# Loading weight tiles, and the queries and keys of attention units, in halves

## The chip, the cores and the metric

The kernel runs on one core of one Trainium2 chip. The metric is the device time of one execution in microseconds (us). It was run three times: 1044.6 us median, 1043.4 to 1045.1. A separate profiled execution gives the trace. Its engines are TensorE (PE in the rows, PEld for its weight loads), VectorE (DVE), ScalarE (ACT), GpSimd (POOL) and SyncE (SP), which here issues the DMA transfers.

## The reference

Attention in chunks over 4 batches, 8 heads, 768 positions and 64 channels a head; its output goes through two feed-forward layers of 3072 tokens, 512 model channels and 2048 hidden ones. All in float32:

```python
for c in range(nc):                      # chunks of 32 queries
    k_full = concat([mem_k, k[l_start:r_end]])   # 8 memory keys, 16 left, 32, 8 right
    scores = scale * q_c @ k_full.T
    a = exp(scores - max(scores)); a = a / (sum(a) + 1e-09)
    out[c] = a @ v_full
x = out as [3072, 512]
h = x @ w_in;  x = (h * clip(h + 3, 0, 6) / 6) @ w_out        # first layer
h = x @ w_in2; out = maximum(0.01 * h, h) @ w_out2            # second layer
```

## The kernel before

Every float32 product of the layers is made of three passes on TensorE: an operand is cut into a high and a low part, and high by high, high by low and low by high are summed. The weights arrive as 64-bit patterns of 128 x 512 numbers (512 KB a tile); "decode" reads one into a "w" buffer in a single transfer (line 393) and rebuilds the float on ACT (line 396) and DVE (lines 400, 404, 408). There are 64 such tiles, 16 for each of the four weight matrices. For much of the work, blocks of 512 tokens are taken in pairs and multiplied in seven products instead of eight, with sums of weights and of tokens that are formed on the way and kept in DRAM ("kept1i", "kept2i", "kept1o", "kept2o").

Attention is done in units: a unit is half a batch of one group of four heads. Its queries and keys come in two transfers of 448 KB (function "load_qk" in "unit", line 491), each with two groups of 96 queries: 128 rows, two runs of 448 numbers in each. The first units of the second half batch are cut into half units (function "half_unit", line 769). The keys are copied into windows (line 341), then follow the scores on TensorE (line 544), the greatest (561), the exponent on ACT (580), the sum (593, 594), the norm on DVE or POOL (598), the transposes on TensorE (602) and the product with the values (622, 634). The first units run before there is anything for the layers; the later ones are placed between matmuls of the first layer.

The order of all this is not written by hand. Each step is a task with a cost per engine, a key, the buffers that it takes and the tasks that it follows. The function "schedule" runs through a model of the engines in time and hands out the tasks; each engine then executes its instructions in the order so found. For a DMA the model books 500 ns of SP for each transfer that the task says it issues ("issues"), at most eight transfers on their way (LANES), and the bytes on one wire. In the built program, too, SP uses eight semaphores in turn (DMAHW0 to DMAHW7): a transfer that takes a semaphore waits for the one eight before it. Buffers are few: "st" has two, "ys" four, "wm" two.

Of the kernel before, what the change touches and what calls it, by code (L numbers as in the profile page):

```python
# [9 lines left out]
F32 = mybir.dt.float32  # L10
F32R = mybir.dt.float32r
U32 = mybir.dt.uint32
# [5 lines left out]
B, H, S, D, NMEM = 4, 8, 768, 64, 8  # L18
# [5 lines left out]
QK = 2 * G + 2 * KW  # L24
# [32 lines left out]
RATE_QK, RATE, RATE_V, COLD = 380.0, 220.0, 300.0, 1.1  # L57
# [198 lines left out]
def tile_attn_moe_moe2(ctx: ExitStack, tc: tile.TileContext, raw, w1i, w1o, w2i, w2o, out):  # L256
    nc = tc.nc
# [24 lines left out]
    def make(b, kind=None):  # L282
        if b.tag in ("hx", "y") and b.tag not in pools:

            (attention if b.tag == "hx" else begin).close()
            pools[b.tag] = (ctx.enter_context(tc.tile_pool(name=b.tag, bufs=places[b.tag], space=PSUM, side="right" if b.tag == "hx" else "left")), [128, 512], F32)
        pool, shape, dt = pools[b.tag]
        if kind is not None:
            shape, dt = kind
        b.t = pool.tile(shape, dt, tag=b.tag, name=b.tag)  # L290
        return b.t
# [20 lines left out]
    def act(n, fixed=90.0):  # L312
        return fixed + 0.855 * n
# [4 lines left out]
    def dve2(n):  # L318
        return 67.0 + 0.523 * n
# [7 lines left out]
    def dma(nbytes, rate=250.0):  # L327
        return nbytes / rate
# [3 lines left out]
    def add(fn, opts, key, **kw):  # L332
        t = Task(fn, opts, key, **kw)
        tasks.append(t)
        return t
# [52 lines left out]
    def decode(src, f, key, early=None, after=(), place="wm", gate=(), late=0, own=True, split=None):  # L388

        t, m = Buf("w"), Buf(place)  # L390

        def load(e):
            nc.sync.dma_start(out=make(t, ([128, 512, 2], U32)).rearrange("p w s -> p (w s)"), in_=src[f])

        def scaled(e):
            nc.scalar.mul(make(m, ([128, 512], F32)), t.t[:, :, 1].bitcast(F32), SCALED)

        def bits(e):
            mu = m.t.bitcast(U32)
            nc.vector.tensor_scalar(out=mu, in0=mu, scalar1=3, scalar2=0x7FFFFFF8, op0=ALU.logical_shift_left, op1=ALU.bitwise_and)  # L400

        def sign(e):
            mu = m.t.bitcast(U32)
            nc.vector.scalar_tensor_tensor(out=mu, in0=t.t[:, :, 1], scalar=0x80000000, in1=mu, op0=ALU.bitwise_and, op1=ALU.bitwise_or)

        def low(e):
            mu = m.t.bitcast(U32)
            nc.vector.scalar_tensor_tensor(out=mu if own else t.t[:, :, 0], in0=t.t[:, :, 0], scalar=29, in1=mu, op0=ALU.logical_shift_right, op1=ALU.bitwise_or)

        k = add(load, {"SP": dma(524288, 380.0)}, key - 30 if early is None else early, after=after, allocs=[t])  # L410
        k = add(scaled, {"ACT": act(512)}, key, after=[k, *gate], allocs=[m], uses=[t], late=late)
        k = add(bits, {"DVE": dve2(512)}, key + 0.2, after=[k], uses=[m], late=late)
        k = add(sign, {"DVE": dve(512)}, key + 0.3, after=[k], uses=[m, t], late=late)
        if split is not None:
            w = Buf("w")
            k = add(lambda e: copy(e, make(w)[:, 0, :], m.t), {"ACT": act(512), "DVE": dve2(512)}, key + 1, after=[k], allocs=[w], uses=[m])
            wbuf[split, f], wtask[split, f] = w, (k,)
        k2 = add(low, {"DVE": dve(512)}, key + 0.4, after=[k], uses=[m, t], late=late)
        return (m, k2) if own else (m, t, k, k2)
# [21 lines left out]
    xbuf, xdone, turn, sent = {}, {}, [], {}  # L441
# [23 lines left out]
    def unit(j, quad, key, tag, own=False, direct=False, loads=None):  # L465


        b, half = divmod(j, 2)
        hps, g0 = slice(2 * quad, 2 * quad + 2), 4 * half
        roomy = j in ROOMY  # L470
        e = Buf("w" if own or roomy else "a")
        qk, kw = ([Buf("w" if own or x and roomy else "a") for _ in range(2)] for x in range(2))
        v = [Buf("w" if own or roomy else "a") for _ in range(2)]
        mx, s = Buf("mx"), Buf("mx")
# [2 lines left out]
        jb, at = divmod(j * NU, N)  # L477
        first = min(NU, N - at)

        def both_groups(hp):  # L480

            a = raw[b, hp, g0, D:, :QK]
            row = a.ap[0][0]
            return bass.AP(tensor=a.tensor, offset=a.offset, ap=[[row, 128], [2 * 128 * row, 2], a.ap[1]])

        def of_raw(par, rows, cols):
            return raw[b, hps, g0 + par:g0 + 4:2, rows, cols]

        def load_qk(i):
            def fn(eng):  # L490
                nc.sync.dma_start(out=make(qk[i], ([128, 2, QK], F32)), in_=both_groups(2 * quad + i))
            return fn

        def load_v(i):
# [217 lines left out]
                sent.setdefault(c, []).append(k)  # L712

        loads = loads or (key - 50, key - 50, key - 38, key - 38)
        l1 = [add(load_qk(i), {"SP": dma(128 * 2 * QK * 4, RATE_QK)}, loads[i], after=() if own else turn, allocs=[qk[i]]) for i in range(2)]
        t = [add(windows(i), ({"DVE": 850.0} if i or quad else {"ACT": 1050.0}) if j == 0 else {"ACT": 1050.0}, key - 30, after=[l1[i]], allocs=[kw[i]], uses=[qk[i]]) for i in range(2)]
        l2 = [add(load_whole(i) if plain else load_v(i), {"SP": dma(128 * 2 * NC * 512, RATE_V if plain else RATE)}, loads[2 + i], after=() if own else t, allocs=[v[i]], issues=3 if plain else 6, loads=plain) for i in range(2)]
        if plain:
# [1 line left out]
        t = marks["s", j, quad] = add(scores, {"PE": (COLD if direct else 1.0) * 1300.0}, key - 16, ins=192, after=t, allocs=[ps], uses=[*qk, *kw])  # L720
        scored = t
        if direct and quad in SHIFT:
            t = add(greatest, {"DVE": 2100.0}, key - 15, after=[t], allocs=[mx, e], uses=[ps])
            t = add(exp_all, {"ACT": act(2 * PAIRS * W)}, key - 13, after=[t], uses=[e])
            t = add(total, {"DVE": 1250.0}, key - 12, after=[t], allocs=[s], uses=[e])
        else:
            t = add(greatest, {"DVE": 1200.0}, key - 15, after=[t], allocs=[mx], uses=[ps])
            t = add(exp(0), {"ACT": 6 * 330.0}, key - 13, after=[t], allocs=[e, s], uses=[ps, mx])
            if not own:
                turn[:] = [scored] if roomy else [t, *l2]  # L730
            t = add(exp(1), {"ACT": 6 * 330.0}, key - 13, after=[t], uses=[ps, mx, e, s])
            t = add(total, {"DVE": 350.0}, key - 12, after=[t], uses=[s])
        t = add(norm, {"DVE": 900.0} if direct else {"POOL": 1800.0, "DVE": 900.0}, key - 11, after=[t], uses=[e, s])
        t = marks["t", j, quad] = add(transpose, {"PE": (COLD if direct else 1.0) * 600.0}, key - 7, ins=12, after=[t], uses=[e, ps])
        t = add(take_p, {"ACT": act(PAIRS * 128)}, key - 5, after=[t], uses=[pt, e])
        t = marks["v", j, quad] = add(values_whole if plain else values, {"PE": (COLD if direct else 1.0) * 1600.0}, key, ins=192, after=[t, *l2], uses=[e, *v, ps])
# [12 lines left out]
    def half_unit(j, quad, gp, key, tag, loads, copies, cold):  # L749


        b, second_half = divmod(j, 2)
        g0 = 4 * second_half + 2 * gp
        qk, kw, v, e = (Buf("w") for _ in range(4))
        mx, s = Buf("mx"), Buf("mx")
# [10 lines left out]
        def load_qk(eng):  # L766
            a = raw[b, hps, g0, D:, :QK]
            there = bass.AP(tensor=a.tensor, offset=a.offset, ap=[[a.ap[1][0], 128], a.ap[0], a.ap[2]])
            nc.sync.dma_start(out=make(qk, ([128, 2, QK], F32)), in_=there)

        def load_v(eng):
            make(v, ([128, 2, NC, 2 * D], F32))
# [169 lines left out]
            if not blk:  # L942
                behind[:] = [a1]

        l1 = add(load_qk, {"SP": dma(128 * 2 * QK * 4, RATE_QK)}, loads[0], allocs=[qk])
        l2 = add(load_v, {"SP": dma(128 * 2 * NC * 512, RATE_V)}, loads[1], allocs=[v], issues=4 if whole else 8, loads=not gp)
        if whole:
            l2 = add(memory, {"POOL": 1500.0}, key - 20, after=[l2], uses=[v])
        t = add(windows, {copies: {"ACT": 1050.0, "DVE": 700.0, "POOL": 1800.0}[copies]}, key - 30, after=[l1], allocs=[kw], uses=[qk])
        t = marks["s", j, quad, gp] = add(scores, {"PE": cold * 650.0}, key - 16, ins=96, after=[t], allocs=banks, uses=[qk, kw])  # L950
        marks["b", j, quad, gp] = banks
        if gp or quad not in SHIFT_HALF:
            t = add(greatest, {"DVE": 700.0}, key - 15, after=[t], allocs=[mx], uses=banks)
            t = add(exp, {"ACT": 6 * 330.0}, key - 13, after=[t], allocs=[e, s], uses=[*banks, mx])
            t = add(total, {"DVE": 350.0}, key - 12, after=[t], uses=[s])
        else:
            t = add(greatest, {"DVE": 1250.0}, key - 15, after=[t], allocs=[mx, e], uses=banks)
            t = add(exp_all, {"ACT": act(2 * NC * W)}, key - 13, after=[t], uses=[e])
            t = add(total, {"DVE": 800.0}, key - 12, after=[t], allocs=[s], uses=[e])
        t = add(norm, {"DVE": 500.0}, key - 11, after=[t], uses=[e, s])  # L960
        t = marks["t", j, quad, gp] = add(transpose, {"PE": cold * 300.0}, key - 7, ins=6, after=[t], uses=[e, *banks])
        t = add(take_p, {"ACT": act(NC * 128)}, key - 5, after=[t], uses=[*banks, e])
        t = marks["v", j, quad, gp] = add(values_whole if whole else values, {"PE": cold * 900.0}, key, ins=96, after=[t, l2], uses=[e, v, *banks])
# [613 lines left out]
    splits, early = [], WEIGHTS  # L1577
    for f in range(KF):
        for which, src, at in (("1i", w1i, pos_h["1", int(f >= KF // 2), f]), ("1o", w1o, pos_y["1", int(f >= KF // 2), f])):
            i = 2 * f + (which == "1o")  # L1580
# [33 lines left out]
    for kind, j, f, *n in seq2:  # L1614
        if kind == "p":
            p, i, n = j, f, n[0]
# [69 lines left out]
```

## Time and profile before

| | us |
|---|---|
| median of the three runs | 1044.6 |
| profiled execution | 1042.63 |
| its span, first to last instruction | 1040.9 |
| TensorE busy in the span | 1030.1 |
| DVE, ACT busy | 855.1, 692.6 |
| mean rate of all DMA | 212 GB/s |

The busy time of TensorE counts pipelined matmuls, whose ends are modelled; a TensorE that is busy in 99% of the span still has places where a matmul waits, and these are read from the waits, not from the share. SP's times are those of issuing a transfer, not of moving its bytes.

### The profile page before, as it was taken

The page shows a single profiled execution, that of the slowest core. Times are in us where ns is not written, and L with a number is a line of the kernel's source. Part 1 is how long each engine was busy: PE and PEld are TensorE (multiplying, and loading weights), DVE is VectorE, ACT ScalarE, POOL GpSimd, SP SyncE. Part 2 cuts the span into 40 slices and gives each one's busy share as a digit, 9 for nine tenths or more (in the row PEclk, how much of TensorE's full clock was granted, in tenths as well). Part 3 has the DMA queues.
Part 4 walks back from the last instruction along what each step waited for, and adds up shares of the span by engine and source line. Part 5 has one row for each costly group of instructions (what it writes and reads, how often), then busy time and mean ns, then how long its engine had stood idle before and what let it go on. Part 6 is the DMA issues. An engine that isn't in the chain of part 4 may idle for free.

```text
span 1040.9 us, 20153 instructions
## 1 busy us (share of the span) xinstructions
PE 1030.1 (99%) x7476; PEld 849.9 (82%) x7476; DVE 855.1 (82%) x1423; ACT 692.6 (67%) x1478; POOL 22.3 (2%) x30
## 2 busy tenths in 40 slices
PE   7999999999999999999999999999999999999998
PEld 4788988888888888888888888888888888888887
DVE  6896897578999887599999898999466998566775
ACT  4896776656888554576786576775565874666753
POOL 4010000000000000000000000000000000000000
PEclk9999999999999999999999999999999999999999
DMA  9889787887897989464638894456342564522451
GB/s 266 297 241 324 258 281 238 254 293 221 286 315 232 328 280 322 157 214 135 215 129 281 268 299 151 152 170 204 128 156 81 182 200 143 179 105 99 144 182 61
DMA packets 127315, 220.50 MB, mean 212 GB/s; under 512 B 12528, under 2 KB 76016, under 8 KB 127216
## 3 DMA queue, kind: packets, MB, share of 16 engines
q1 hardware_dynamic: 127216, 219.20, 63.1%
q8 instruction: 59, 0.97, 0.4%
q14 instruction: 40, 0.33, 0.1%
HBM read 156.24 MB, written 62.91 MB: 211 GB/s over the span
## 4 chain that ended last, share of the span: by engine, by line
PE 96%; DMA 1%; DVE 1%; ACT 1%; issue 0%; SPq 0%; ACTq 0%; DVEq 0%
PE y L1322 17%; PE y L1047 15%; PE y L1490 13%; PE h L1322 11%; PE h L1490 8%; PE hx L1490 8%; PE hx L1322 8%; PE h L998 8%; PE h L1047 2%; PE at L634 2%; DMA w<-in_raw 1%; PE at L544 1%; PE at L602 1%; PE ac L461 1%; ACT w L845 0%; PE at L622 0%
## 5 line engine op out<-in xcount | busy, mean ns | idle before, releaser
L344 DVE TENSOR_TENSOR w<-w 128x512 fp32r<-128x512 f32 (+2 forms) x407 | 333.4, 858 | 28.6 <-ACT w L341 28.2
L341 ACT CAST w<-w 128x512 fp32r<-128x512 f32 (+1 forms) x296 | 226.5, 799 | 16.6 <-DMA w<-floats 7.2
L1322 PE MATMUL y<-w 128*128 128x512 f32 x516 | 124.5, 390 | 0.0
L1047 PE MATMUL y<-g,w 128*128 128x512 f32 (+1 forms) x540 | 124.4, 374 | 0.0
L1322 PEld LDWEIGHTS y<-w 128*128 128x128 f32 x516 | 96.7, 188 | 19.9
L1047 PEld LDWEIGHTS y<-g,w 128*128 128x128 f32 x540 | 94.2, 189 | 17.3
L341 ACT CAST g<-w 128x512 fp32r<-128x512 f32 x80 | 49.7, 622 | 67.6 <-PE y L1490 22.3
L1490 PE MATMUL y<-w 128*128 128x512 f32 x384 | 90.3, 389 | 0.0
L1490 PEld LDWEIGHTS y<-w 128*128 128x128 f32 x384 | 72.1, 188 | 14.9
L1296 ACT ACTIVATE w<-w 128x512 f32<-128x512 f32 x72 | 45.2, 631 | 43.0 <-DVE w L1289 21.5
L344 DVE TENSOR_TENSOR g<-w,g 128x512 fp32r<-128x512 f32 x80 | 54.8, 694 | 14.6 <-ACT g L341 14.4
L998 PE MATMUL h<-xh,w 128*128 128x512 f32 (+1 forms) x288 | 66.0, 370 | 0.0
L1490 PE MATMUL h<-w 128*128 128x512 f32 x264 | 62.1, 389 | 0.0
L1490 PE MATMUL hx<-w 128*128 128x512 f32 x252 | 59.2, 389 | 0.0
L1322 PE MATMUL h<-xl,w 128*128 128x512 f32 x240 | 58.2, 390 | 0.0
L1490 PEld LDWEIGHTS h<-w 128*128 128x128 f32 x264 | 49.6, 188 | 10.2
L998 PEld LDWEIGHTS h<-xh,w 128*128 128x128 f32 x288 | 49.7, 189 | 8.9
L1490 PEld LDWEIGHTS hx<-w 128*128 128x128 f32 x252 | 47.3, 188 | 9.8
L1322 PEld LDWEIGHTS h<-xl,w 128*128 128x128 f32 x240 | 44.9, 188 | 9.3
L1322 PE MATMUL y<-xh,w 128*128 128x512 f32 x216 | 52.0, 390 | 0.0
L1367 DVE TENSOR_TENSOR w<-y,w 128x512 f32<-128x512 f32 x35 | 24.0, 691 | 29.7 <-PE y L1322 26.9
L1322 PEld LDWEIGHTS y<-xh,w 128*128 128x128 f32 x216 | 40.5, 188 | 8.4
(243 smaller groups left out, 1836.5 us busy)
## 6 DMA issues: line engine op xcount, KB each, us to landing
w<-kept2i SPq DMA_DIRECT2D x42, 512.0 KB
w<-kept2o SPq DMA_DIRECT2D x42, 512.0 KB
w<-kept1i SPq DMA_DIRECT2D x28, 512.0 KB
a<-in_raw SPq DMA_DIRECT2D x20, 448.0 KB
w<-in_w1i SPq DMA_DIRECT2D x16, 512.0 KB
w<-in_w1o SPq DMA_DIRECT2D x16, 512.0 KB
w<-in_w2i SPq DMA_DIRECT2D x16, 512.0 KB
w<-in_w2o SPq DMA_DIRECT2D x16, 512.0 KB
```

Of the source, the lines that this page charges most:

```text
L341: nc.scalar.copy(out, in_) if e == "ACT" else engine(e).tensor_copy(out=out, in_=in_)
L344: engine(e).tensor_tensor(out=out, in0=a, in1=b, op=ALU.subtract)
L461: nc.tensor.matmul(x, ident, ident.unsqueeze(1).to_broadcast([128, c, 128]), start=True, stop=True, skip_group_check=True)
L544: nc.tensor.matmul(ps.t[h * CHUNK:(h + 1) * CHUNK, par, i * W:(i + 1) * W], qk[h // 2].t[r, gp, (h % 2) * G + c * CHUNK:(h % 2) * G + (c + ...
L602: nc.tensor.transpose(pt.t[:, i // NC, (i % NC) * 128:(i % NC + 1) * 128], pview()[:, i * 128:(i + 1) * 128], ident)
L634: nc.tensor.matmul(pv.t[(h % 2) * D:(h % 2 + 1) * D, par, (h // 2) * 2 * G + i * CHUNK:(h // 2) * 2 * G + (i + 1) * CHUNK], v[h // 2].t[r, ...
L998: nc.tensor.matmul(h.t[:, o:o + n], w.t[:, 1 if p == 1 else 0, k * 128:(k + 1) * 128], x[:, k, c0:c0 + n], start=(p == 0 and k == 0 and o ...
L1047: nc.tensor.matmul(bank(banks[d])[:, c0:c0 + n], w.t[:, 1 if p == 1 else 0, d * 128:(d + 1) * 128], g.t[:, 1 if p == 2 else 0, at:at + n], ...
L1296: return add(lambda e: nc.scalar.activation(out=at(), in_=at(), func=AF.Prelu, alpha=0.01), {"ACT": act(N)}, key, after=[after], uses=uses)
L1322: nc.tensor.matmul(bank(to), wt(l, o)[:, kt * 128:(kt + 1) * 128].bitcast(F32R), operand(p, name, 1 if q == 2 else 0, kt).bitcast(F32R), s ...
L1367: done[2] = add(lambda e: nc.vector.tensor_tensor(out=half_of(x, 0), in0=bank(bb), in1=ut.t[:, 0], op=ALU.add), low, key, after=[k, done[1 ...
L1490: nc.tensor.matmul(bank(to[d]), wt(1 if q == 1 else 0, o)[:, d * 128:(d + 1) * 128].bitcast(F32R), g.t[:, 1 if q == 2 else 0], start=(fres ...
```

## The change

A weight tile comes in two transfers of 128 rows by 2048 bytes, 256 of its 512 columns each, into the same buffer. The queries and keys that came as one transfer of two runs per row come as two transfers of one run per row, in whole and in half units. The tasks tell the planner that they issue two transfers ("issues=2") of the same bytes in all. The readers of the tiles are unchanged.

```diff
@@ decode
         def load(e):
-            nc.sync.dma_start(out=make(t, ([128, 512, 2], U32)).rearrange("p w s -> p (w s)"), in_=src[f])
+            make(t, ([128, 512, 2], U32))
+            for x in (0, 256):
+                nc.sync.dma_start(out=t.t[:, x:x + 256].rearrange("p w s -> p (w s)"), in_=src[f, :, 2 * x:2 * x + 512])
...
-        k = add(load, {"SP": dma(524288, 380.0)}, key - 30 if early is None else early, after=after, allocs=[t])
+        k = add(load, {"SP": dma(524288, 380.0)}, key - 30 if early is None else early, after=after, allocs=[t], issues=2)
@@ unit
-        def both_groups(hp):
-
-            a = raw[b, hp, g0, D:, :QK]
-            row = a.ap[0][0]
-            return bass.AP(tensor=a.tensor, offset=a.offset, ap=[[row, 128], [2 * 128 * row, 2], a.ap[1]])
+        def both_groups(hp, gp):
+
+            a = raw[b, hp, g0 + 2 * gp, D:, :QK]
+            return bass.AP(tensor=a.tensor, offset=a.offset, ap=[[a.ap[0][0], 128], a.ap[1]])
...
-                nc.sync.dma_start(out=make(qk[i], ([128, 2, QK], F32)), in_=both_groups(2 * quad + i))
+                make(qk[i], ([128, 2, QK], F32))
+                for gp in range(2):
+                    nc.sync.dma_start(out=qk[i].t[:, gp], in_=both_groups(2 * quad + i, gp))
...
-        l1 = [add(load_qk(i), {"SP": dma(128 * 2 * QK * 4, RATE_QK)}, loads[i], after=() if own else turn, allocs=[qk[i]]) for i in range(2)]
+        l1 = [add(load_qk(i), {"SP": dma(128 * 2 * QK * 4, RATE_QK)}, loads[i], after=() if own else turn, allocs=[qk[i]], issues=2) for i in range(2)]
@@ half_unit
-            nc.sync.dma_start(out=make(qk, ([128, 2, QK], F32)), in_=there)
+            make(qk, ([128, 2, QK], F32))
+            for i in range(2):
+                nc.sync.dma_start(out=qk.t[:, i], in_=bass.AP(tensor=a.tensor, offset=there[:, i].offset, ap=[there.ap[0], there.ap[2]]))
...
-        l1 = add(load_qk, {"SP": dma(128 * 2 * QK * 4, RATE_QK)}, loads[0], allocs=[qk])
+        l1 = add(load_qk, {"SP": dma(128 * 2 * QK * 4, RATE_QK)}, loads[0], allocs=[qk], issues=2)
```

The new file is longer: line 491 of before is 494 of the new file, 544 is 547, 602 is 605, 634 is 637, 998 is 1003, 1047 is 1052, 1322 is 1327.

SP at the start of the program, before. The names are buffers and inputs; "waits" tells whose semaphore a transfer needs:

```order
L491 DMA w<-in_raw 128x2x448 x4
L512 DMA w<-in_raw 128x4x128
L514 DMA w<-in_raw 64x2x128 x2
L769 DMA w<-in_raw 128x2x448
L512 DMA w<-in_raw 128x4x128 [waits DMAHW0_49]
L514 DMA w<-in_raw 64x2x128 [waits DMAHW1_49]
L514 DMA w<-in_raw 64x2x128 [waits DMAHW2_49]
L769 DMA w<-in_raw 128x2x448 [waits DMAHW3_49]
L512 DMA w<-in_raw 128x4x128 [waits DMAHW4_49]
```

And the same place now:

```order
L494 DMA w<-in_raw 128x448 x8
L515 DMA w<-in_raw 128x4x128 [waits DMAHW0_49]
L517 DMA w<-in_raw 64x2x128 [waits DMAHW1_49]
L517 DMA w<-in_raw 64x2x128 [waits DMAHW2_49]
L774 DMA w<-in_raw 128x448 [waits DMAHW3_49]
L774 DMA w<-in_raw 128x448 [waits DMAHW4_49]
L515 DMA w<-in_raw 128x4x128 [waits DMAHW5_49]
L517 DMA w<-in_raw 64x2x128 [waits DMAHW6_49]
L517 DMA w<-in_raw 64x2x128 [waits DMAHW7_49]
L774 DMA w<-in_raw 128x448 [waits DMAHW0_49]
L774 DMA w<-in_raw 128x448 [waits DMAHW1_49]
```

The first unit's four loads take eight semaphores where they took four, so the first unit's values (line 512, now 515) are the ninth transfer and the first that waits; the second half unit's queries and keys (line 769, now 774) were the twelfth and wait now, as seventeenth and eighteenth, for the ninth and tenth. The loads before and behind keep their sequence.

TensorE around the unit whose scores stood at 200 us in the trace, before. "at" is the PSUM tile of attention, "h" and "y" those of the layer:

```order
L544 MATMUL at<-w,a 32x64 x48
L998 MATMUL h<-xl,w 128x512 x4
L1047 MATMUL y<-g,w 128x512 x12
L998 MATMUL h<-xh,w 128x512 x8
L998 MATMUL h<-xl,w 128x512 x4
L602 MATMUL at<-ident,w 128x128 x6
```

And now:

```order
L547 MATMUL at<-w,a 32x64 x48
L1052 MATMUL y<-g,w 128x512 x4
L1003 MATMUL h<-xh,w 128x512 x8
L1003 MATMUL h<-xl,w 128x512 x4
L1052 MATMUL y<-g,w 128x512 x12
L1003 MATMUL h<-xh,w 128x512 x8
L605 MATMUL at<-ident,w 128x128 x6
```

Between the scores and the transposes stood 28 matmuls of 512 columns; now 36 do (4 + 8 + 4 + 12 + 8).

TensorE around the unit whose scores stood at 279 us, before:

```order
L544 MATMUL at<-a 32x64 x48
L1322 MATMUL y<-xl,w 128x512 x6
L1322 MATMUL h<-w 128x512 x12
L1322 MATMUL y<-xl,w 128x512 x12
L1322 MATMUL h<-w 128x512 x12
L1322 MATMUL y<-w 128x512 x4
L602 MATMUL at<-ident,a 128x128 x6
```

And now:

```order
L547 MATMUL at<-a 32x64 x48
L1327 MATMUL y<-xl,w 128x512 x10
L1327 MATMUL h<-w 128x512 x12
L1327 MATMUL y<-xl,w 128x512 x12
L1327 MATMUL h<-w 128x512 x8
L605 MATMUL at<-ident,a 128x128 x6
```

46 matmuls stood between; now 42 do. The norm of this unit stays on POOL. Of the four units from 250 us on, three had the norm on POOL, and now all four have; of the five before them, the first had it on POOL, and now none has.

## Rows read from the trace of the kernel before

**Rows 1.** The page's header

```profile
span 1040.9 us, 20153 instructions
```

**Rows 2.** TensorE's waits from 44 us to the end

```profile
PE at L602 <- DVE w L598: 0.9, 1, 0.9
PE at L894 <- ACT w L341: 0.6, 1, 0.6
```

**Rows 3.** The chain that ended last: start us, us, what

```profile
8.07 7.63 DMA w<-in_raw
...
504.23 10.88 PE hx L1490 x48
```

**Rows 4.** Groups by line: the decodes' first step, ACT

```profile
L396 ACT ACTIVATE wm<-w 128x512 f32<-128x512 f32 x40 | 26.8, 679 | 3.0 <-DVE ys L1208 2.5 <-DMA kept2o<-wm 0.4
```

**Rows 5.** Stretches: engines' busy us, granted clock, DMA share, GB/s

```profile
3.50:7.00 3.50, 3.32 (x51) 1.18 (x56) 0.97 (x5) 1.11 (x4) 0.00 (x0) 1.00 1.05 392
25.50:30.00 4.50, 4.50 (x46) 3.96 (x44) 3.08 (x8) 2.30 (x6) 0.86 (x2) 0.50 1.01 402
...
24.00:28.00 4.00, 4.00 (x93) 3.94 (x90) 2.58 (x5) 0.99 (x4) 2.24 (x4) 0.50 0.97 376
28.00:32.00 4.00, 4.00 (x64) 3.16 (x65) 2.53 (x6) 2.35 (x5) 0.00 (x0) 0.69 1.00 319
```

**Rows 6.** Timeline of the lead-in: start us, us, what, idle before

```profile
0.74 1.97 SPq L491 DMA_DIRECT2D w<-in_raw  x4
...
4.39 1.11 ACT L341 COPY w<-w 128x336 f32<-128x336 f32 x4 [2.17 <-DMA w<-in_raw]
...
8.07 0.37 SPq L769 DMA_DIRECT2D w<-in_raw  x1
...
9.36 0.37 SPq L512 DMA_DIRECT2D w<-in_raw  x1
```

**Rows 7.** Timeline of TensorE, scores and transposes of attention units

```profile
143.56 1.17 PE L544 MATMUL at<-w,a 64*32 64x64 f32 x96
...
200.29 1.17 PE L544 MATMUL at<-w,a 64*32 64x64 f32 x96
...
208.98 0.85 PE L602 MATMUL at<-ident,w 128*128 128x128 f32 x6 [0.95 <-DVE w L598]
...
279.28 1.17 PE L544 MATMUL at<-a 64*32 64x64 f32 x96
...
290.95 0.82 PE L602 MATMUL at<-ident,a 128*128 128x128 f32 x6
...
307.09 1.17 PE L544 MATMUL at<-a 64*32 64x64 f32 x96
...
330.37 1.17 PE L544 MATMUL at<-a 64*32 64x64 f32 x96
```

**Rows 8.** Timeline of DVE, norms of these units

```profile
152.25 0.96 DVE L598 TENSOR_TENSOR w<-w,mx 128x768 f32<-128x768 f32 x1
...
207.88 0.96 DVE L598 TENSOR_TENSOR w<-w,mx 128x768 f32<-128x768 f32 x1
...
314.59 0.96 DVE L598 TENSOR_TENSOR a<-a,mx 128x768 f32<-128x768 f32 x1
```

**Rows 9.** Timeline of POOL, norms of these units

```profile
289.29 1.48 POOL L598 TENSOR_TENSOR a<-a,mx 128x768 f32<-128x768 f32 x1 [26.76 <-DMA w<-in_w2i]
338.54 1.57 POOL L598 TENSOR_TENSOR a<-a,mx 128x768 f32<-128x768 f32 x1 [47.77 <-DMA a<-in_raw]
```

**Rows 10.** DMA issues from 160 to 200 us, two of nine rows

```profile
w<-in_w2i SPq DMA_DIRECT2D x4, 512.0 KB
a<-in_raw SPq DMA_DIRECT2D x4, 448.0 KB
```

**Rows 11.** DVE's waits from 120 to 345 us

```profile
DVE st L1189 <- DMA kept1i<-st: 1.6, 1, 1.6
```

**Rows 12.** TensorE's waits before 44 us

```profile
PE ac L461 <- ACT w L845: 2.0, 1, 2.0
```

## The prediction

> **What bounds the kernel now.** I read the page's header and its first table, then TensorE's waits before and after 44 us, the chain that ended last, the stretches, and last the timelines of single places. The span is 1040.9 us [rows 1]; the profiled execution took 1042.63 us, so 1.7 us lie outside the span, and the median of the three timed runs, 1044.6, is 2.0 above that execution. I work in changes to the profiled execution and add 2.0 at the end.
>
> From 44 us to the end TensorE waits twice: 0.6 us at the attention matmul of line 894 and 0.9 us at the transposes of line 602 [rows 2]. Everything else there is matmul against matmul, at the pace of 10.88 us for 48 matmuls of 512 columns, 0.2267 us each [rows 3]. So some 993 us are TensorE's own work, which the change leaves as it is: the same 4188 matmul-equivalents of 512 columns stand in both orders. Only two things can move the time: the lead-in before 44 us, which is loads, softmax and a few small matmuls, and new or vanished waits behind it. No engine on TensorE's path is held up by a weight: of the 40 decodes into "wm" that read a loaded weight tile, none waited for its load (the 3.0 us before them are put down to DVE and to a store) [rows 4].
>
> **What is added.** 64 weight loads, 28 loads of queries and keys of whole units and 4 of half units become two each: 96 more DMA issues on SP, and nothing computed is more or less. Every consumer still needs both halves, so no work can start on the first one.
>
> *Bytes.* A row of a weight transfer shrinks from 4096 to 2048 bytes; the rows of queries and keys stay 1792 bytes. Where SP's loads with 1792-byte and 512-byte rows ran alone they moved 392 GB/s, where weights ran almost alone 402 [rows 5]. So 2048-byte rows cost at most 2.5% more engine time: 0.03 us on the 1.3 us of a 512 KB tile, 0.4 us over the dozen tiles issued in the lead-in. The decodes above hide that; without this cover it would be 0.4 us.
>
> *The lead-in's queue.* SP issues four loads in 1.97 us, 0.49 each [rows 6]. At most eight are out: the ninth waits for the semaphore of the first, and so on in turn (the first order piece). The eight halves now take 3.9 us to issue where four loads took 1.97. Their data is the limit, though: the first load is first used at 4.39, and the fourth has landed at 8.07 us, when the issue that waits for it goes [rows 6]; that is 1.23 us per 448 KB, so halves issued every 0.49 us (0.61 us of data each) keep ahead of it. What moves is the half unit's load of queries and keys on the chain that ended last, from 8.07 us for 7.63 us [rows 3]: it was twelfth, issued when the fourth load had landed. As seventeenth and eighteenth its halves wait for the ninth and tenth transfers, the first unit's values, whose landing freed the issue at 9.36 [rows 6]: 1.3 us later. Ahead of it in the queue lie then 832 to 960 KB issued and not landed, at 392 GB/s 2.2 to 2.5 us. The first load took 3.65 us from its issue to its use, 1.23 of them data, so 2.42 us pass before a load needs the engines: the queue just covers that, and the load keeps its place in the stream. Bounds: 0 if so, +1.3 if the queue runs dry; I take what is short, half of 0.2, +0.1. Every instruction of TensorE, DVE, ACT and POOL stands in the same order up to about 120 us, so the lead-in holds no other edit.
>
> [...]
>
> *The attention units between 131 and 346 us.* The planner books two issues and so places these units anew. A unit is a chain: scores on TensorE (line 544), greatest, exponent, sum and norm on DVE, ACT and DVE or POOL (line 598), transposes on TensorE (602). TensorE never waits if the other matmuls between 544 and 602 last longer than the chain. From the end of 544 to the end of 598 it takes 8.48 us for the unit at 143.56, 7.38 at 200.29, 7.29 at 307.09, all with the norm on DVE; with it on POOL 10.32 at 279.28 and 8.57 at 330.37 [rows 7 to 9]. TensorE goes on 0.14 to 0.18 us later.
>
> The one wait of 0.95 us is the unit at 200.29: 28 matmuls stood between, 28 x 0.2267 = 6.35 us, too few for 7.38. Now 36 stand there, 8.16 us (second order piece): the wait goes, -0.95. What is late next is the other units. Counted in the new order, the spacings of the five units from 131 to 210 us are 38, 40, 36, 36, 36 (8.61, 9.07 and three times 8.16 us), and of the four later ones 42, 42, 44, 44 (9.52 and 9.97 us), where 46, 46, 36, 42 stood; all four now have the norm on POOL. Best case: no wait. Worst: the three at 36 each need 8.48 + 0.14, 0.46 short each, 1.4; the late four each need 10.32 + 0.16, short by 0.96, 0.96, 0.51, 0.51, 2.9; together +4.3. The unit at 307.09 ran with 36 and without a wait, which is the row nearest to the early ones: nothing. For the late ones I take the mean of the two POOL rows, 9.45 + 0.16 = 9.61: 0.09 short twice, +0.2; and 0.3 more since the greatest and the sum queue behind other DVE work that now stands elsewhere. New waits: +0.5, bounds 0 and +4.3.
>
> *SP behind the lead-in.* Between 160 and 200 us SP issues 66 transfers (nine rows summed, two of which are those that the change doubles, 4 and 4) [rows 10]. Eight more take 3.9 us of SP's 40. I cost them at nothing: TensorE's side of those loads had time to spare throughout [rows 2, 4]. If that cover goes, see the first rival.
>
> **Sum.** +0.1 - 0.95 + 0.5 = -0.35: 1042.63 becomes 1042.3, and with the 2.0 of the median 1044.3 us.
>
> **Rivals.**
> First, slower: SP becomes the bound from 160 to 210 us. It issues in order, and behind each half stand stores that free the "st" and "ys" buffers; DVE already waits 1.6 us for such a store [rows 11], in the same queue from which softmax is served. A delay of 3.9 us decides once it passes a unit's spare time, 8.16 - 7.29 - 0.14 = 0.7 us; then TensorE loses 3.2 us, and 6.4 if the next unit still has the delay: +2.9 to +6.1 on the forecast, 1047.2 to 1050.4. Eight lanes at 3.65 us each pass 2.19 transfers per us; (66 + 8)/40 = 1.85 are wanted, so it should just hold. Against it: no wait of TensorE in that stage is for a load. 17%.
>
> Second, the spacings of the late units are too short on POOL: the worst case above, +3.8 on the forecast, 1048.1; half of it 1046.4. For it: all four on POOL, and one POOL row at 10.32. Against: the planner holds spacing by the same booked times as before. Beyond +0.2% of the median: 8%.
>
> Third, faster: TensorE's clock. [...] Half or more of it, or the wait at 200 us gone with a better lead-in: 16%.
>
> Fourth, the change is not felt at all because each late load was hidden and the waits balance: that is the forecast within its own width, 1042.9 to 1046.3.
>
> **How the numbers follow.** What a measurement of this kernel can tell from no change is about 0.2%, 2.1 us. The forecast and the fourth case together lie within it: 59%. Slower by more are the first two, 17 + 8 = 25%; faster the third, 16%. Eight times in ten: down to 1041.0 (the third), up to 1049.0 (the second whole, most of the first).
>
> **What would show it.** Right: TensorE's waits from 44 us lose the 0.9 us at line 602 near 200 us and show a few tenths at other transposes; the small matmuls at 23 us start within 0.5 us of before; the doubled loads show no longer waits of ACT's decodes. The first rival would show waits of TensorE of 3 us and DVE waiting for stores of "st" and "ys"; the second, waits at line 605 of the new file behind POOL between 250 and 345 us; the third, a granted clock of 1.00 from 24 to 32 us. A lead-in more than 1.3 us longer, or a wait of TensorE for a weight, would make the prediction wrong in a step that I cost at nothing.

## The result, and the profile after

The changed kernel took 1053.35 us, median of five runs (1052.13 to 1054.52); before, in five runs, took 1044.25 (1043.4 to 1045.1). The ratio is 1.0082, with a 95% interval of 1.0068 to 1.0096: 7 to 10 us slower. The prediction was 1044.3, with a range up to 1049.0, and slower had a chance of 25%. The measured time lies above the range.

Differences in us below are (ratio - 1) x 1044, their intervals likewise. "TensorE's shift" is the start of a matmul after, less the start of the same matmul in the profile of before; the orders of the two kernels agree on TensorE up to 131 us of before, and again from 346 us on.

The header of the page after, to be held against [rows 1]:

```profile
span 1051.5 us, 20280 instructions
```

The span is 10.6 us longer. TensorE's waits of after from 44 us to the end (line, what it waited for, us in total, times, longest) answer to [rows 2]:

```profile
PE y L1052 <- ACT g L341: 1.6, 1, 1.6
PE at L605 <- POOL w L601: 0.8, 1, 0.8
PE at L899 <- ACT w L341: 0.6, 1, 0.6
PE h L1327 <- DVE w L1294: 0.5, 1, 0.5
PE at L547 <- ACT a L341: 0.4, 2, 0.2
PE at L637 <- ACT w L341: 0.4, 1, 0.4
PE y L1052 <- DVE g L344: 0.4, 1, 0.4
PE at L547 <- issue: 0.3, 1, 0.3
PE at L871 <- DVE w L867: 0.2, 1, 0.2
```

The wait of 0.9 us at the transposes near 200 us is gone, as forecast. The 0.6 us at line 899 (894 in before) stood in before too; the other eight rows, 4.6 us together, are new. Of these, 3.5 us lie between 81 and 122 us, where before had none. By TensorE's shift, at times of after: 1.4 us at 7.4 us, 3.9 at 44 us, 5.0 at 81, 6.3 at 93, 8.7 at 122, 7.8 behind 200 us (the wait that went), 9.1 at 355 and 9.7 from 644 us on.

The lead-in in TensorE's timeline of after (start us, us, what, idle before and its releaser):

```profile
5.07 0.43 PE L547 MATMUL at<-w 64*32 64x64 f32 x4
7.44 1.91 PE L547 MATMUL at<-w 64*32 64x64 f32 x92 [1.94 <-DVE w L341]
```

Four scores run at 5.07 us, the other 92 wait for windows that are copied from the second load; before ran all 96 from 5.07 us on. TensorE's waits of after before 44 us, which answer to [rows 12]:

```profile
PE ac L463 <- ACT w L850: 2.0, 1, 2.0
PE at L547 <- DVE w L341: 1.9, 1, 1.9
PE ac L463 <- POOL three L307: 1.4, 1, 1.4
PE h L816 <- issue: 0.9, 1, 0.9
PE ac L816 <- DVE w L341: 0.7, 1, 0.7
```

The 1.9 us of these scores are new. The 2.0 and 1.4 us at line 463 (461 in before) stood in before too, and line 816 (811) waited there twice for 0.6 us.

Stretches of after (busy us of each engine, then granted clock, DMA share, GB/s), which answer to [rows 5]:

```profile
3.50:7.00 3.50, 2.00 (x6) 0.25 (x5) 0.05 (x1) 1.11 (x4) 0.00 (x0) 1.00 0.89 240
24.00:28.00 4.00, 2.89 (x36) 2.06 (x38) 2.34 (x6) 2.16 (x10) 1.54 (x3) 0.50 0.86 220
28.00:32.00 4.00, 4.00 (x82) 3.84 (x78) 0.81 (x3) 1.35 (x5) 0.88 (x2) 0.50 0.91 319
32.00:36.00 4.00, 4.00 (x74) 3.26 (x74) 2.14 (x5) 1.85 (x5) 0.00 (x0) 0.68 0.82 242
```

SP's loads now moved 240 GB/s from 3.5 to 7 us, where before had 392 [rows 5]. The granted clock of TensorE was 0.50 from 17.5 to 34.6 us, in before from 23.7 to 30.5, and 1.00 on either side; it fell behind waits of TensorE of 0.9 and 0.7 us at 15 and 17 us, where before, with 0.65 and 0.63 us, kept 1.00 up to its wait of 2.0 us at 22 us. What makes it fall is not shown. While after ran at 0.50 and before still at 1.00, TensorE's shift grew from 1.2 us to 3.6.

Now SP. These rows were not read for the prediction, and they are the ones that count. SP's timeline of before: the first weight of a run of six, the unit's queries and keys within it, its last weight, and the loads of the next two units.

```profile
40.34 0.36 SPq L393 DMA_DIRECT2D w<-in_w1o  x1
...
42.21 1.20 SPq L491 DMA_DIRECT2D w<-in_raw  x2
...
44.05 0.39 SPq L393 DMA_DIRECT2D w<-in_w1o  x1
...
57.48 0.91 SPq L491 DMA_DIRECT2D w<-in_raw  x2
...
69.96 0.91 SPq L491 DMA_DIRECT2D a<-in_raw  x2
```

The same places in SP's timeline of after:

```profile
44.82 0.82 SPq L395 DMA_DIRECT2D w<-in_w1o  x2
...
48.91 2.60 SPq L494 DMA_DIRECT2D w<-in_raw  x4
...
53.72 1.14 SPq L395 DMA_DIRECT2D w<-in_w1i  x2
...
63.82 1.77 SPq L494 DMA_DIRECT2D w<-in_raw  x4
...
78.08 1.77 SPq L494 DMA_DIRECT2D a<-in_raw  x4
```

These eight loads went out in 4.1 us (40.34 to 44.44); now they are 16 transfers and take 10.0 (44.82 to 54.86). Of the 10 us by which the last one ends later, 4.5 stand at the first already and the rest arises within the run. The units' loads start 6.3 and 8.1 us later than in before, while TensorE at 44 us is only 3.9 late. ACT copies these queries and keys into windows. Its wait for them in before, from 56 to 82 us:

```profile
ACT w L341 <- DMA w<-in_raw: 0.8, 1, 0.8
```

And in after, from 60 to 90 us:

```profile
ACT w L341 <- DMA w<-in_raw: 4.5, 2, 2.4
ACT w L341 <- DMA a<-in_raw: 1.4, 2, 0.9
```

0.8 us became 5.9. Already in before one of these copies waited for its load: the loads came just in time, and [rows 4], which hold the decodes of weights into "wm" alone, do not show it. In ACT's order of instructions the softmax of the unit before stands behind these copies, and while ACT waits for them it is held up too: its exponents start at 74.56 us, in before at 67.68, 6.9 us earlier; behind them come the norm on POOL and TensorE's wait for it at 81 us (line 605), then a wait for a copy of ACT at 86 us (line 637).

The wait of 1.6 us at line 1052, at 120 us, has another load of SP's queue behind it, a store. SP sends the stores "half<-ys", which free the buffers "ys", behind the weights; in before, then in after:

```profile
94.47 2.59 SPq L1088 DMA_DIRECT2D half<-ys  x4
106.08 2.64 SPq L1093 DMA_DIRECT2D half<-ys  x4
```

ACT waits for one of them before it can go on with a weight, in before and in after:

```profile
ACT ys L396 <- DMA half<-ys: 1.1, 1, 1.1
ACT ys L398 <- DMA half<-ys: 3.8, 1, 3.8
```

Halves are not needed for this wait, as the last paragraph on the prediction shows.

### The profile page after: what moved, and what is told of

Same layout as the page of the kernel before. It is cut to its first block, busy times and chain, and to the rows that moved or that the text cites. A ratio compares the mean times of both kernels' runs of the same rounds, so it can differ in the third digit from the quotient of the medians.

```text
span 1051.5 us, 20280 instructions
## 1 busy us (share of the span) xinstructions
PE 1035.1 (98%) x7476; PEld 851.3 (81%) x7476; DVE 853.0 (81%) x1423; ACT 692.7 (66%) x1478; POOL 20.2 (2%) x30
## 4 chain that ended last, share of the span: by engine, by line
PE 82%; DMA 9%; SPq 3%; DVE 3%; issue 1%; ACT 1%; ACTq 0%; DVEq 0%
PE y L1327 14%; PE y L1052 13%; PE y L1495 12%; PE h L1327 9%; PE h L1495 8%; PE hx L1495 8%; PE hx L1327 7%; PE h L1003 6%; DMA w<-in_raw 3%; PE h L1052 2%; PE at L637 2%; SPq L395 1%; PE at L547 1%; DMA attended<-a 1%; DMA kept2o<-ys 1%
```

## Experiments

All are variants of before. Where "order of before" stands, TensorE, DVE, ACT and, but for transfers put on it, GpSimd have exactly before's sequence of instructions.

### Transfers or order, weights or queries and keys

*split_old_order*: the changed kernel with the planner told nothing.

```diff
-... key - 30 if early is None else early, after=after, allocs=[t], issues=2)
+... key - 30 if early is None else early, after=after, allocs=[t])
```

(and the same for both loads of queries and keys)

> All 96 loads in two as in the change, but the planner books one issue each, so that TensorE, DVE, ACT and POOL work in the order of before. Theory A (later data: the doubled transfers make loads land later, in the lead-in and again between 50 and 120 us): the lead-in is some 4 us longer, TensorE idles about 3.5 us more between 80 and 125 us, and the wait of 0.9 us near 200 us is back: slower than before by 8 to 11 us, 1053 to 1056. Theory B (the new order of the attention units costs the time): within 2 us of before, 1043 to 1046.

Measured: 1051.68 us, ratio 1.0066 [1.0047, 1.0085], +6.9 us, a little below the range of theory A.

*whole_new_order*: the reverse, issues=2 for the same three loads, in whole transfers.

> The loads of before, one transfer each, but the planner books two issues, so that TensorE, DVE, ACT and POOL work in the order of the changed kernel. Theory A (later data): the wait near 200 us is gone and a few tenths stand at the late units: within 1 us of before, 1043.3 to 1045. Theory B (the order): slower than before by 7 to 10 us, 1051 to 1054.

Measured: 1044.04, ratio 0.9991 [0.9978, 1.0004]. The transfers alone carry the loss; the new order, which takes away the 0.9 us wait and adds small ones, costs nothing that can be told. Theory A holds, B falls.

*weights_only* has only the edits in "decode", *qk_only* only those of queries and keys, each with its issues=2; TensorE's order is that of after up to 285 us in the first and that of before up to 262 us in the second; behind that each has its own.

> Only the 64 weight tiles are loaded as two transfers. Theory A1 (each doubled transfer delays by its own turn of a semaphore, wherever it stands): weights are 64 of the 96, of which some 10 stand in the first 45 us, where the 12 loads of queries and keys stand too: the lead-in keeps its first 17 us of before and is 1 to 2.5 us longer at 44 us, the whole 4 to 6 us slower, 1048 to 1050. Theory A2 (only the queries and keys, on which the chain of the lead-in hangs, cost): within 1.5 us of before, 1043 to 1046.

> Only queries and keys are loaded as two transfers, of whole and of half units. Theory A1 (every doubled transfer): the scores of the first unit start 1.3 us later as in the changed kernel, the lead-in is 1.5 to 3 us longer, the whole 3 to 5 us slower, 1047 to 1049. Theory A2 (only these cost): 7 to 10 us slower, 1051 to 1054.

Measured: weights alone 1048.62, ratio 1.0037 [1.0026, 1.0049], +3.9; queries and keys alone 1050.95, ratio 1.0055 [1.0035, 1.0074], +5.7. Both count, so A2 falls. A1 is right in kind. The weights came out near the lower end of its 4 to 6 us, the queries and keys above its 3 to 5; by the medians 32 of these loads cost more than 64 weights, though the intervals overlap. The rows of queries and keys are 1792 bytes in both kernels, so their loss cannot come from shorter rows.

### Where

Three kernels split only the loads of a stretch, in the order of before; the loads are numbered as SP issues them.

```diff
-                nc.sync.dma_start(out=make(qk[i], ([128, 2, QK], F32)), in_=both_groups(2 * quad + i))
+                if not halved():      # r <= 22; 22 < r <= 45; r > 45; in first4: r <= 3
...
```

> In the order of before, only the 23 loads of weights, queries and keys that before issues up to 44.05 us go in two. Theory L (the lead-in's queue: the eight turns are used up there, SP falls behind, and all later loads with it): nearly all of the loss, 5 to 8 us slower than before, 1049 to 1052. Theory P (each doubled load costs at its own place, the units at 57 and 70 us most): the scores at 6 us start 1.3 us later, 1 to 3 us in all, 1045 to 1047.

> In the order of before, only the 23 loads that before issues from 57 to 124 us go in two. Theory L: within 1.5 us of before, 1043 to 1046. Theory P: 3 to 6 us slower, 1047 to 1050, with TensorE's waits at the transposes and probabilities of 76 to 87 us and at the squares of 112 us.

> In the order of before, only the 50 loads from 134 us on go in two. Both theories: within 1.5 us of before, 1043 to 1046, with the 0.9 us wait near 200 us. Slower than 1047 would say that the first rival of the prediction (SP as the bound from 160 to 210 us) has a share after all.

Measured: 1.0022 [1.0006, 1.0038], +2.3; 1.0007 [0.9992, 1.0022], +0.7; 0.9994 [0.9977, 1.0011], -0.6. The 50 loads behind 125 us cost nothing that can be told, so the first rival, which put its bound at 160 to 210 us, shows no share. (One profile of split_from125 has 1.4 us of waits for ACT at 215 us; the times do not show them.) The other two together give 3.0 where the whole split gives 6.9, and neither theory had that: L wanted 5 to 8 from the first, P 3 to 6 from the second. So the loss seems to be more than the sum of its places, which fits slack being used up: SP is made late before 44 us, and halves behind it turn that into waits. The intervals are wide, though.

*first4* splits the first four loads alone:

> Order of before; only the first four loads (queries and keys of the two units that open the lead-in) go in two. If their third half again lands some 1.5 us after the first of its parts, TensorE's second half of the scores starts at 7.3 us instead of 6.1. Theory F (this alone sets the lead-in): 1 to 2 us slower than before, 1045 to 1047. Theory L (the lead-in loses by the many turns behind them): the shift is made up by 17 us, within 1 us of before.

Measured: 1.0010 [1.0001, 1.0019], +1.0, on the border between the two. The 92 scores started at 6.21 us, not 7.3: the lag of the third half was there (parts landed 4.29 to 5.01 us), but smaller than after, 4.31 to 6.24.

### What a transfer costs

*sp_events*: whole transfers, and work for SP alone.

```diff
+def pause(nc):
+    for n in range(8):
+        nc.sync.sem_inc(TICK[0], 1)
...
             nc.sync.dma_start(out=make(qk, ([128, 2, QK], F32)), in_=there)
+            pause(nc)
```

> Loads and order of before, whole transfers; behind each of the 96 loads SP also counts a semaphore up eight times, which nobody waits for: some 0.4 us of SP's time, about what one more issue takes, without a transfer and without a turn of the eight semaphores. Theory I (SP's own time for issuing is what delays the loads): 5 to 8 us slower than before, 1049 to 1052. Theories L (the eight turns) and R (shorter rows): within 1.5 us of before, 1043 to 1046.

Measured: 1.0041 [1.0026, 1.0056], +4.3 us, in the gap between the two expectations. A pause took 0.5 us of SP. By the medians SP's own time makes some 60% of the loss; the intervals allow a third of it, and all of it. In its trace the run of eight loads starts at 40.3 us as in before and its last weight goes at 47.2 instead of 44.05. That execution was the fastest of the six (1045.96) and has no wait of TensorE between 81 and 93 us, so it does not show where the time goes.

*uneven*: two transfers each, the second next to nothing.

```diff
-            for x in (0, 256):
+            for lo, hi in ((0, 504), (504, 512)):
```

> Order of before; each of the 96 loads goes in two, but unevenly: 504 and 8 of the 512 columns of a weight, 432 and 16 of the 448 of queries and keys, so that the first transfer is nearly the whole one, with rows of 4032 and 1728 bytes, and the second next to nothing. Theories L and I (a transfer costs its turn and its issue, whatever it carries): as the even split in this order, 1049 to 1053. Theory R (shorter rows, 97 ns for 2048 bytes against 182 for 4096, cost the engines time): within 2 us of before, 1043 to 1046.5.

Measured: 1.0074 [1.0058, 1.0090], +7.7: as much as the even split, so nothing was won with rows of 4032 bytes. Rows of 2048 bytes did cost more, 97 ns a packet (mean of all of that size in the first 125 us of after) against 182 for 4096 (before), some 7% more per byte. But uneven does not by itself decide between number and length: a row of a weight now took a packet of 187 ns and one of 64 bytes of 11, 198 ns in all, no less than the 195 of two halves. What speaks against theory R is qk_only above, whose rows did not change, and sp_events, which has no packet more.

*rows64* splits by partitions, 64 and 64, and keeps rows of 4096 bytes:

```diff
+                nc.sync.dma_start(out=t.t[lo:hi]..., in_=src[f, lo:hi])      # (0, 64), (64, 128)
```

> In the order of before, all 96 loads go in two by partitions, 64 and 64, so that a row of a weight stays 4096 bytes long. Theory N (the number of transfers: SP's issues and the eight semaphores): as the split by columns in this order, 1050 to 1054. Theory B (shorter rows cost the DMA engines time): within 1.5 us of before, 1043 to 1046.

Measured: 1081.91, ratio 1.0343 [1.0314, 1.0372], +36 us, which neither theory has. Two stretches of its trace (columns as above) show why it says nothing on their dispute:

```profile
44.00:60.00 16.00, 15.18 (x223) 12.10 (x224) 13.27 (x33) 11.63 (x35) 0.00 (x0) 1.00 0.88 201
60.00:80.00 20.00, 16.20 (x201) 12.81 (x201) 14.24 (x28) 12.46 (x38) 0.00 (x0) 0.91 0.94 210
```

The DMA engines are busy 88 to 94% for 201 to 210 GB/s, where before moved 273 and 298 at 83 and 92%. A packet of 1792 bytes took 120 ns (median) instead of 74, and in the first 125 us one of 4096 bytes 264 instead of 159. It is the packets of the split loads that became slower; those of 512 bytes, of loads that were not split, only went from 27 to 33 ns. Why is not shown.

### SP's queue relieved

*two_queues* gives the second half of each load to GpSimd's queue:

```diff
-            for x in (0, 256):
-                nc.sync.dma_start(
+            for x, q in ((0, nc.sync), (256, nc.gpsimd)):
+                q.dma_start(
```

> Order of before; all 96 loads in halves as in the change, but the second half of each is issued by GpSimd on its own queue, so that SP issues as many transfers as before, in the same order and with the same turns of its eight semaphores. Theories L and I: within 2 us of before, 1042 to 1046.5, if GpSimd's transfers land no later than SP's. Theory R: 1049 to 1053, as the halves have the same rows as in the change.

Measured: 1.0081 [1.0060, 1.0101], +8.5, against theories L and I by its total. By place it is not a clean test: GpSimd sent large loads out of turn (a weight's half at 4.8 us, the next at 15.4, behind copies), TensorE's shift is 4.1 us by 39 us of before, and 6.5 us are added from 210 us on, first waits of 1.8 us for ACT, then 10.2 us at a lower granted clock (its mean over the execution is 0.988). But from 44 to 138 us, where SP issued no more than in before, the shift grew by 0.8 us, against 4.8 in after from 44 to 113 us of before.

*mem_pool* and *split_mem_pool* move small transfers instead, those of the eight memory rows. The traces have 56 of them, 48 of units (24 KB each) and 8 of half units (12 KB); where the expectations say 64 and 16, and 32 transfers more, it is 56, 8 and 40:

```diff
-                    nc.sync.dma_start(out=v[i].t[par * D:par * D + NMEM]...
+                    nc.gpsimd.dma_start(out=v[i].t[par * D:par * D + NMEM]...
...
-                    nc.sync.dma_start(out=v.t[par * D:par * D + NMEM, i], ...
+                    nc.gpsimd.dma_start(out=v.t[par * D:par * D + NMEM, i], ...
```

> Loads of before in whole transfers, and its order on TensorE, DVE and ACT; only the 64 small transfers that fetch the eight memory rows of values go to GpSimd's queue. Theory Q (SP's queue: its issues and its eight turns delay the loads): SP has 64 issues fewer; before waits little for loads, so the gain is small: 0 to 2.5 us faster, 1041 to 1044. Rival R (DMA engines' time per byte): no change within 1 us.

> All 96 loads in two by columns, the order of before, and the 64 small transfers of memory rows on GpSimd's queue: SP issues 32 transfers more than before instead of 96 more, 44 of the 64 having stood before 200 us. Theory Q: most of the 7 us comes back, 1044 to 1047. Rival R: as the split in this order without it, 1050 to 1053.

Measured: 1.0018 [1.0007, 1.0028], +1.9, and 1.0026 [1.0013, 1.0039], +2.7. With these transfers off SP the split adds 0.8 us instead of 6.9 by the medians, as theory Q wants, and ACT's waits for the units' loads, 5.2 us from 56 to 92 us in split_old_order, are gone. SP's rows of split_mem_pool stand as the ones above:

```profile
39.56 0.83 SPq L395 DMA_DIRECT2D w<-in_w1o  x2
...
44.80 2.04 SPq L494 DMA_DIRECT2D w<-in_raw  x4
...
48.54 1.51 SPq L395 DMA_DIRECT2D w<-in_w1o  x2
...
56.86 1.77 SPq L494 DMA_DIRECT2D w<-in_raw  x4
...
70.59 2.00 SPq L494 DMA_DIRECT2D a<-in_raw  x4
```

56.86 and 70.59: back at the times of before. That mem_pool itself lost was a miss. In TensorE's timeline of mem_pool the values of a half unit stop halfway:

```profile
36.00 0.56 PE L882 MATMUL ac<-w 64*64 64x32 f32 x20
39.18 0.70 PE L882 MATMUL ac<-w 64*64 64x32 f32 x28 [2.62 <-issue]
```

The memory rows that were moved are not the reason: line 882 does not read them, and the last of those issued up to then had landed at 37.70 us. The profile names no releaser ("issue"). What it has is a packet of 16 KB of the DMA queue "instruction", which in before ended at 34.20 us and here at 37.84; the section at the end comes back to such packets. TensorE thus probably waited for its own instructions, which no run tests; why they came later is open. In split_mem_pool the same wait is 0.2 us, so mem_pool is no clean base for the 0.8 us.

*new_order_mem_pool* is mem_pool with the order of after:

> Whole transfers, the order of the changed kernel on TensorE, DVE and ACT, and the 64 small transfers on GpSimd's queue: the two edits that cost nothing or gave a little, together. Theory Q: 1 to 3 us faster than before, 1041 to 1043. Rival R: as the new order alone, 1043 to 1045.

Measured: 1.0024 [1.0011, 1.0038], +2.5: a miss by the same wait (3.2 us in its trace).

The last three move the 48 of the units alone:

> Whole transfers, order of before on TensorE, DVE and ACT; only the 48 small transfers of memory rows of the units go to GpSimd's queue, the 16 of the half units stay on SP. If the 1.9 us of the move of all 64 came from the half units' values: the wait of 2.6 us at 39 us is gone, 1042.5 to 1045. If GpSimd's queue as such costs: again some 2 us slower than before, 1045.5 to 1047.5.

> The same move with all 96 loads in two, order of before. Theory Q (SP's queue): the 2 to 3 us that the split costs in the lead-in stay, as SP's queue is as full there as in the split alone, and the loss between 44 and 125 us is gone: 1046 to 1048.5. If the small transfers of the half units were what mattered: 1050 to 1053 as the split alone.

> Whole transfers, the order of the changed kernel, and the 48 small transfers of the units on GpSimd's queue: the candidate for a version that beats both kernels. Theory Q: 0.5 to 2.5 us faster than before, 1041.5 to 1043.5; if the queue of SP holds nothing up in before, the same as before within 0.5 us.

Measured: 1.0001 [0.9983, 1.0019]; 1.0073 [1.0048, 1.0098], +7.6; 0.9987 [0.9974, 1.0000], -1.4. So by the medians the 1.9 us went with the eight transfers of the half units. And the split is as dear as alone, the second of the two expectations: what relieved SP were those eight, between 25 and 42 us. SP's timeline of split_unit_mem_pool shows it late again:

```profile
43.81 0.82 SPq L395 DMA_DIRECT2D w<-in_w1o  x2
...
47.88 2.11 SPq L494 DMA_DIRECT2D w<-in_raw  x4
...
61.30 2.73 SPq L494 DMA_DIRECT2D w<-in_raw  x4
...
74.14 1.82 SPq L494 DMA_DIRECT2D a<-in_raw  x4
```

The lateness is thus made by the loads that before sends up to 44 us, where half units, weights and units share SP's queue, and carried to the units at 57 and 70 us. It is not shown that these loads are what costs the time here: in this trace TensorE waits 1.6 us at 58 us for softmax, 1.1 at 100 us for ACT and 2.3 at 108 us without a releaser in the profile, then has a lower granted clock for 3.4 us (its mean over the execution is 0.995). The last kernel, at 1042.55 us against 1043.89 beside it, is the fastest of all here; its interval just touches before.

## Why the prediction was wrong

- *TensorE bounds from 44 us on, so only the lead-in and waits can move the time*: right. The loss lies before 44 us and, as waits, from 81 to 122 us, with a little from 270 to 355 us. (The 4188 matmuls of 512 columns are 4200 in both traces; nothing hangs on it.)
- *Bytes, shorter rows cost at most 2.5%*: some 7% in the mean (97 ns for 2048 bytes, 182 for 4096). It does not decide: qk_only, with rows of the same length, lost 5.7 us.
- *The lead-in's queue, +0.1, bounds 0 and +1.3*: wrong, the first failed step. I let halves issued every 0.49 us keep ahead of their data. They were issued in time (every 0.47 us), but the parts of the third landed between 4.31 and 6.24 us, and the fourth load was whole at 9.37 us instead of 8.06. The half unit's load was issued at 10.54 us instead of 8.07, not 1.3 us later but 2.5. TensorE's shift was 1.2 us at 15 us, within the bounds, and 3.9 at 44 us, beyond them. Most of what lies between is the clock of this execution, as the section on the profile shows: split_old_order, whose granted clock from 20 to 44 us had the mean of before, 0.86 (after 0.70), had 0.8 at 44 us and 2.1 from 57 us on.
- *The unit at 200 us, -0.95*: right, the wait is gone, and 36 matmuls stand where 28 stood.
- *New waits at other units, +0.5*: within its bounds. From 267 to 346 us of before the shift grows by 1.2 us, with waits for windows that ACT copies (line 547) and for an addition on DVE (line 1294) where I had named norms. Over the whole, the order alone is at -0.9 us.
- *SP behind the lead-in, nothing*: the step that made the prediction wrong. From 160 to 200 us it held (split_from125, -0.6 us). But I had tested one stretch, and from waits of TensorE and of one kind of decode I concluded that loads "had time to spare throughout". A missing wait says that a load was not late, not how early it was. Between 24 and 57 us SP's queue had none to spare (eight loads that went out in 4.1 us took 10.0), and the copies of queries and keys had hardly any (one waited 0.8 us already in before). Of the 5.8 us by which the shift of after grows behind 44 us, 2.4 come from 81 to 93 us, most of it behind these copies, and 2.4 at 120 us, where ACT had waited for a store from the same queue. Of the whole loss sp_events puts some 60% on SP's own time (4.3 of 6.9 to 7.7 us by the medians); the rest goes with the turns of the eight semaphores, or with whatever else a transfer costs its queue, which no run here parts.
- *Rivals*. The first had the right mechanism, SP as the bound, at the wrong place (160 to 210 instead of 24 to 80 us), with a price of +2.9 to +6.1 for its stage. Its stores behind the halves are seen too, at 106 us, with ACT and not DVE waiting for them. The second does not show: no wait for GpSimd behind 250 us. The third did not come: after was granted 0.50 for longer than before. No run shows the gain from it that the range's lower end, 1041.0, takes in, 3.3 us under the forecast. What the runs show is less: over 118 runs of before next to these kernels the 15 with a granted clock of 1.000 have a mean of 1043.1 us, the 10 with 0.992 one of 1046.2, 0.4 us for each 0.001 (a correlation: waits like those of 0.9 and 0.7 us ahead of the fall in after are in it), so from the 0.997 of the profiled execution of before up to 1.000 some 1.2 us. The five runs of after have a mean of 0.994 against 0.996: some 0.7 us of the 9.1.
- *96 more DMA issues on SP*: the kernel with them, in transfers of 224 and 256 KB, took 9.1 us more, 0.09 us for each.

Open: transfers (+6.9) and order (-0.9) add up to 6.0, with their intervals some 3.6 to 8.4, and after lost 7 to 10. The wait of TensorE for ACT at line 1052 (1047 in before), near 113 us of before, is part of that. Waits of 1.1 to 2.0 us stand in the profiles of after and of split_old_order, whole_new_order, qk_only, split_to44 and split_from125; in all six ACT had waited 3.2 to 4.2 us for a store "half<-ys". In before and in five variants with at most 0.3 us of it (weights_only, split_44_125, uneven, first4, two_queues) ACT had waited 0.9 to 2.4 us; in the three kernels with all 56 small transfers on GpSimd neither wait is there. So the wait hangs on how late SP's queue sends that store. But split_from125 and whole_new_order have only whole loads up to there, so it also comes without the change; how often in each kernel, single profiles don't tell. Nor does the change alone make the waits for copies: whole_new_order, with TensorE 2.1 us ahead, has one of 3.0 us, behind which TensorE did not wait.

## What to carry to other kernels

Before a transfer is cut in two, read the issuing engine's own timeline where its queue is fullest, and the first consumer of every kind of load: ACT's one wait of 0.8 us for queries and keys, harmless in before, said that the slack was zero, and it became 5.9. The added transfers on SP's full queue delayed the loads and stores behind them, the loads of two units by 6.3 and 8.1 us; the same split cost 2.3 us in the loads up to 44 us and nothing that can be told in those behind 125 us, and ACT waited 3.8 us, where before had 1.1, for a store that was not split. Test a split with one that keeps the length of the rows and with a pause of the issuing engine (here +5.7 and +4.3 us): the two tell count from bytes.

## What was not expected of the hardware

- Transfers of 64 partitions cost packets of 1792 bytes 120 ns instead of 74, and the kernel 36 us; the split by columns, with the same number of bytes and transfers, cost 7.
- With halves of queries and keys first in the queue, the parts of one transfer land up to 1.9 us apart (4.31 to 6.24 us) where those of whole ones land 0.4 apart (3.93 to 4.37). Two packets of 1.4 and 1.1 us stand at 3.6 and 4.2 us of after; why they come there is open.
- Eight increments of a semaphore on SP behind each of 96 loads cost the kernel 4.3 us, though no engine waits for them.
- In the twenty profiles here TensorE has 36 waits of more than 0.15 us behind 2 us for which the profile names no releaser ("issue"). Every one of them ends 1.2 to 1.6 us behind the end of a packet of 16 KB of the DMA queue "instruction" (q8 of the page); the wait of 0.9 us at 15.33 us of after, for one, ends 1.37 us behind a packet that ended at 13.96. That TensorE then waits for its own instructions, brought by that queue, is the likely reading; no run tests it.
